# A spectral filter followed by a gated feed-forward network on one core: fifteen blocks of the down-projection rewritten with seven products, and the filter's middle stage re-timed

## The chip, the core and the metric

The kernel runs on one NeuronCore of a Trainium2 chip. TensorE (PE, with its weight loads shown as PEld) multiplies matrices into PSUM, VectorE (DVE), ScalarE (ACT) and GpSimd (POOL) work on tiles, and SyncE (SP) and POOL issue most of the DMAs. The metric is the time of one execution in device microseconds; a lower time is better. The median of three runs of the kernel before is 863.33 us (863.15 to 863.42).

## The reference

Two layers follow each other. The first multiplies the spectrum of each sequence by a filter; the second normalizes every row and applies a gated feed-forward network.

```python
batch, seq, dim = (8, 3008, 256);  n_tokens, d_model, d_ff = (24064, 256, 1536)

X = np.fft.rfft(x, axis=1)
Y = X * (filt_r + 1j * filt_i)[None, :, :]
x = np.fft.irfft(Y, n=3008, axis=1).reshape(24064, 256)

rms = np.sqrt(np.mean(x * x, axis=-1, keepdims=True) + 1e-06)
xn = x / rms * rms_g
g = xn @ w_gate
silu = g * (1.0 / (1.0 + np.exp(-g)))
out = silu * (xn @ w_val) @ w_out
```

## The kernel before

**The feed-forward part sets the frame.** There are 8 sequences `b`, each of 6 blocks `m` of 512 tokens (the last block of a sequence has 384 or 512), and each block takes 12 steps `jt`, one for every 128 columns of d_ff. Such a step is a *slot*; there are 576, numbered through as `items`. In slot `i`, `gv` (L533) makes the gate product in `pg` and the value product in `pv`, each as two accumulating matmuls of 512 columns (L546). ACT applies Silu to `pg` and writes `sg` (L550); DVE multiplies `pv` by `sg` and writes `hh`, 128 d_ff columns by 512 tokens in fp16 (L551). Two slots later `down` (L554) multiplies `hh` by the 128 rows of `wo` of this step: four matmuls, one for each 128 tokens, with the tokens' `hh` as weights and 256 columns of `wo` moving (L563). They accumulate over the 12 steps in two PSUM banks, `po0` and `po1`. After the last step ACT copies one bank and DVE the other to `o3` (L568, L569), and SP stores it. The first `down` of a block is put off by one slot, so that the banks can be emptied.

`pg` and `pv` have two PSUM banks each, `hh` four buffers, `po0` and `po1` one each.

**The filter part runs in the gaps.** For sequence `b` it has these units:

- `x_load` (POOL issues the DMA), `a_unit` (a 512-column matmul into `psa`, copied by ACT or DVE), `z_store` and `t2_load` (SP): the first stage.
- The *middle stage*, sixteen units `i` of each sequence: `b_unit` (four 96-column matmuls into `psb`, L241, and a DVE multiplication by the filter, `s_part`, L231), one slot later the second `s_part` (L234), another slot later `add_unit` (POOL adds both to `ss`, L268); after every second one `yt_load` (a transposing DMA from SP), and some slots later `bi_unit` for both (four 96-column matmuls into `psi`, L285, copied by ACT).
- `t4_load` (SP, transposing), `n_unit` (a 512-column matmul into `psn`, L314, copied by ACT), `sq_unit` (ACT squares and sums, L322), `stat_unit` and `xt_unit` (POOL, L330 to L340), `tr_unit` (SP, transposing) deliver the `xn` of a block.

The first sequence goes through its own start-up, with transposes by TensorE in place of DMAs (`psy`, L418), and one block whose scale is split in two fp16 parts by DVE (`hl`, L509 and L510).

**A planner written in Python sets the order.** For each unit it takes a list of wished slots and `fit` pushes a unit later until the PSUM bank ("M" or "B") is free and the planned loads of ACT ("A") and DVE ("V") leave room. What is planned for a slot is issued behind that slot's `gv` and in front of the `down` of two slots earlier; every engine works through its own queue in that order. For the sequences 3 to 7 the middle stage's wishes are, with `t = (b - 1) * 72`:

```python
b_at, lags, soft = [t - (25 if b == 3 else 26) + 4 * i for i in range(16)], (8, 12), ()
```

The two lags say how many slots behind the `b_unit` the two `bi_unit`s go.

**Staging buffers.** A pool `stg` of four 8 KB buffers per partition holds the filter (`f_load`) and the weights (`w_load`) at the start, and afterwards the `y` tiles of the norm, which use half of a buffer.

Of the kernel before, what the change touches and what calls it, by code (L numbers as in the profile page):

```python
# [10 lines left out]
FP32 = mybir.dt.float32  # L11
FP16 = mybir.dt.float16
AXT = mybir.ActivationFunctionType
ALU = mybir.AluOpType
# [6 lines left out]
P = 128  # L21
D = 256
B = 8
DFF = 1536
JT = DFF // P
# [8 lines left out]
XC = 6  # L34
NXC = H // XC
KC = 8


def _make_tables():
# [62 lines left out]
def kernel(  # L102
# [11 lines left out]
    nc = tc.nc  # L114
# [6 lines left out]
    z_d = nc.dram_tensor("z_tmp", (B, K2, KR, D), FP16, kind="Internal").ap()  # L121

    glob = ctx.enter_context(tc.tile_pool(name="glob", bufs=1))
    stg = ctx.enter_context(tc.tile_pool(name="stg", bufs=4))
    xp = ctx.enter_context(tc.tile_pool(name="xp", bufs=4))
    t1p = ctx.enter_context(tc.tile_pool(name="t1p", bufs=3))
    t2p = ctx.enter_context(tc.tile_pool(name="t2p", bufs=3))
# [7 lines left out]
    hp = ctx.enter_context(tc.tile_pool(name="hp", bufs=4))  # L135
    op = ctx.enter_context(tc.tile_pool(name="op", bufs=2))
# [15 lines left out]
    wg = glob.tile([P, 2, DFF], FP16)  # L152
    wv = glob.tile([P, 2, DFF], FP16)
    wo = glob.tile([P, JT, D], FP16)
    gsb = glob.tile([P, 2], FP32)
    hhs = [glob.tile([P, 512], FP16, name="hh%d" % i) for i in range(4)]
    ss3 = [glob.tile([P, 4, 2, P], FP16, name="ss%d" % i) for i in range(3)]
# [9 lines left out]
    def raw(src, row, ap):  # L167
        return bass.AP(tensor=src.tensor, offset=src.offset + row * D, ap=ap)

    def y_tile():  # L170
        t = stg.tile([P, 2, 4, 256], FP32, tag="stg", name="y")
        return t.rearrange("p a b c -> p (a b c)")[:, 0:1024].rearrange("p (a e) -> p a e", a=2)

    def x_load(b, c):
        t = xp.tile([P, XC, D], FP16, tag="xc", name="xc")
# [195 lines left out]
        copy(eng, st[0]["t2"][c][:, 4 * r:4 * r + 4, :].rearrange("p k (e d) -> p k e d", e=2), ps)  # L371

    fst = {}
    FR4 = 4

    def f_load(i, f):
        if i not in fst:
            fst[i] = stg.tile([P, 2, FR4, D], FP32, tag="stg", name="fs")
        t = fst[i]
        row = FR4 * P * i if i < 2 else NF - 1 - FR4 * P  # L380
        for src in ((filt_i, filt_r)[f],):
            nc.gpsimd.dma_start(t[:, f].rearrange("p a d -> p (a d)"),
                                raw(src, row, [[FR4 * D, P], [1, FR4 * D]]))

    def f_unit(i, f, dh, e):
        t = fst[i]
        ps = bank(1 + "AV".index(e), "psf").rearrange("p (a q) -> p a q", a=FR4)
        for a in range(FR4):
            nc.tensor.transpose(ps[:, a, :], t[:, f, a, ds(dh * P, P)], idf)  # L389
# [123 lines left out]
    def scale_apply(m, bk):  # L513
# [12 lines left out]
                                    in1=y[:, h, :].rearrange("p (q e t) -> p q e t", q=2, e=2), op=ALU.mult)  # L526
        st[0]["xn"][m] = xn

    SPLIT = ((0, 0, 0), (B - 1, 5, JT - 1))
    hh_of = {}  # L530
    po_of = {}

    def gv(b, m, jt):  # L533
        n = nq(b, m)
        xn = st[b]["xn"][m]
        parts = ((0, 2), (2, 4)) if (b, m, jt) in SPLIT else ((0, n),)
        sg = hp.tile([P, 512], FP16, tag="sg", name="sg")
        hh = hhs[(6 * JT * b + JT * m + jt) % 4]
        made = []
        for q0, q1 in parts:  # L540
            w = (q1 - q0) * P
            pg = psG.tile([P, 512], FP32, tag="pg", name="pg")
            pv = psV.tile([P, 512], FP32, tag="pv", name="pv")
            for ps, wt in ((pg, wg), (pv, wv)):
                for dt_ in range(2):
                    nc.tensor.matmul(ps[:, 0:w], wt[:, dt_, ts(jt, P)], xn[:, q0:q1, dt_, :],  # L546
                                     start=(dt_ == 0), stop=(dt_ == 1))
            made.append((pg, pv, w, slice(q0 * P, q1 * P)))
        for pg, pv, w, c in made:
            nc.scalar.activation(out=sg[:, c], in_=pg[:, 0:w], func=AXT.Silu)  # L550
            nc.vector.tensor_tensor(out=hh[:, c], in0=pv[:, 0:w], in1=sg[:, c], op=ALU.mult)  # L551
        hh_of[(b, m, jt)] = hh

    def down(b, m, jt):  # L554
        hh = hh_of.pop((b, m, jt))
        if jt == 0:
            po_of[(b, m)] = [psO.tile([P, 2, D], FP32, tag="po%d" % i, name="po%d" % i)
                             for i in range(2)]
        po = po_of[(b, m)]

        n = nq(b, m)
        for s4 in range(n):
            nc.tensor.matmul(po[s4 // 2][:, s4 % 2, :], hh[:, ts(s4, P)], wo[:, jt, :],  # L563
                             start=(jt == 0 and s4 % 2 == 0),
                             stop=(jt == JT - 1 and (s4 % 2 == 1 or s4 == n - 1)))
# [23 lines left out]

    def w_load(q):  # L590
        cols = ts(q, DFF // 3)
        t = stg.tile([P, 2, 2, DFF // 3], FP32, tag="stg", name="ws")
# [17 lines left out]
    with tc.manual_schedule():  # L610
# [18 lines left out]
        w_load(1)  # L629
        nc.vector.memset(mhalf, -0.5)  # L630
        nc.vector.memset(ones, 1.0)
        for t in ss3[1:]:
# [29 lines left out]
        for g in range(7):  # L662
            tr0_unit(g, "V")
            if g < 6:
                f_unit(*todo[g + 2], "A")
        f_neg(4, 4, (0,))
        f_neg(8, 8, (0,))
        UN = K2 // 2
# [54 lines left out]
        for i in range(JT + 1, len(items), JT):  # L723
            load["A"][i] = 0.6
            load["V"][i] = 0.68

        def at(slot, fn, *a):
            todo = (late if fn == q_unit else plan).setdefault(slot, [])
            if fn in front:
                todo.insert(0, (fn, a))  # L730
            else:
                todo.append((fn, a))
# [77 lines left out]
        for b in range(1, B):  # L810
            t = (b - 1) * 72
            if b == 1:
                z = a_plan(b, [i for i in range(12)])
                b_at, lags = [z + 7 + 7 * i // 5 for i in range(16)], (9, 9)
                soft = range(2, 16, 4)
            elif b == 2:
                z = a_plan(b, [28 + 3 * i for i in range(12)])
                b_at, lags, soft = [z + 13 + 7 * i // 3 for i in range(16)], (8, 9), ()
            else:
                at_ = [72 + 3 * i if b == 3 else t - 87 + 4 * i for i in range(12)]  # L820
                z = a_plan(b, [s - (s % JT == 1) for s in at_])
                b_at, lags, soft = [t - (25 if b == 3 else 26) + 4 * i for i in range(16)], (8, 12), ()
            assert z + 3 <= b_at[0] - 4
            end = b_plan(b, b_at, lags, soft)
            for c in range(4):
                at(end + 1 + (3 * c if b < 3 else c), t4_load, b, c)
            n_at = end + (4, 6, 8)[b] if b < 3 else t + (53 if b == 3 else 51)
            assert n_at >= end + 4
            for m in range(6):
                norm_plan(b, m, (n_at + 8 * m, n_at + 8 * m + (4 if b > 1 else 2)), (2, 3, 7) if b > 1 else (2, 3, 6))  # L830

        for i, now in plan.items():
            if any(fn == a_unit and a[3] == 0 for fn, a in plan.get(i + 1, ())) and bi_unit in [fn for fn, _ in now]:
                now.sort(key=lambda u: u[0] == sq_unit)

        stores = {}
        for i in range(len(items) + 4):
            if i < len(items):
                gv(*items[i])
            for fn, a in plan.pop(i, ()):  # L840
                fn(*a)
            if 2 <= i < len(items) + 2:
                b, m, jt = items[i - 2]
                if jt == 1 and i > JT:
                    down(b, m, 0)
                if jt or i < JT:
                    down(b, m, jt)
                if items[i - 2][2] == JT - 1:
                    stores[i + 1] = items[i - 2][:2]
# [35 lines left out]
```

## Time and profile before

| what | value |
|---|---|
| median of 3 runs (lowest, highest) | 863.33 us (863.15, 863.42) |
| span of the profiled execution, first to last instruction | 861.4 us |
| mean granted TensorE clock in it | 0.999 |
| PE busy | 852.4 us (99%) |
| PEld busy | 532.2 us (62%) |
| ACT busy | 612.4 us (71%) |
| DVE busy | 557.2 us (65%) |
| POOL busy | 297.8 us (35%) |
| blocks 3 of sequences 2 to 6, from first gate matmul to first gate matmul | 16.3 us, in sequence 6 16.1 |
| blocks 4 of sequences 2 to 6 | 16.9, 17.2, 17.2, 16.9, 16.3 us |
| blocks 0 to 4 of sequence 7 | 16.0, 16.3, 15.6, 15.6, 15.6 us |

The span comes from one execution under the profiler, for which no time beside its span is given; the runs' median lies 1.9 us above that span. Busy times are unions over all instructions of an engine; matmuls are pipelined and a record shows a matmul from its start to its modelled end, so the pace of TensorE is read from the starts of successive matmuls. In the groups of instructions a row gives the line, engine, operation, tiles and shapes, the count, busy time and mean nanoseconds of one, and the idle time of the engine in front of them with what ended it. In the timeline a row gives the start and the length in us.

### The profile page before, as it was taken

To read this page: it belongs to the slowest core of one execution; us is meant where nothing else is said; L and a number is where in the kernel's file an instruction comes from. 1 tells how busy PE (TensorE), PEld (TensorE's weight loads), DVE (VectorE), ACT (ScalarE), POOL (GpSimd) and SP (SyncE) were. 2 spreads that over 40 slices of the span, in tenths; PEclk is the share of its full clock that TensorE was granted. 3 is DMA by queue.
4 is the path that set the end of the run, shared out by engine and by line. 5 is a ranking of instruction groups with operands and counts; after the bars stand their busy time and mean duration, and the time that the engine had idled before them with its cause. 6 is when DMAs were issued, how large, how long until landed. Compare 5 with 4: busy or idle time off the path is not lost.

```text
span 861.4 us, 17024 instructions
## 1 busy us (share of the span) xinstructions
PE 852.4 (99%) x6142; PEld 532.2 (62%) x6142; DVE 557.2 (65%) x926; ACT 612.4 (71%) x1339; POOL 297.8 (35%) x346
## 2 busy tenths in 40 slices
PE   8999999999999999999999999999999999999997
PEld 6755666566666666666666666666666666665664
DVE  5857655776666666666666676767666665555554
ACT  4986777787588756887577856888567765777443
POOL 5725742453144322534034430444123430132000
PEclk9999999999999999999999999999999999999999
DMA  9995778765975476656755548433564331521101
GB/s 283 270 204 124 150 164 168 139 130 121 197 137 129 121 150 111 151 107 147 139 127 113 132 98 180 108 87 101 131 127 93 97 70 42 124 54 49 62 25 50
DMA packets 198237, 107.98 MB, mean 125 GB/s; under 512 B 158566, under 2 KB 182520, under 8 KB 198152
## 3 DMA queue, kind: packets, MB, share of 16 engines
q1 hardware_dynamic: 189464, 85.52, 44.1%
q0 software_dynamic: 8544, 21.24, 12.7%
q8 instruction: 48, 0.79, 0.4%
q14 instruction: 37, 0.30, 0.1%
q10 hardware_dynamic: 144, 0.13, 0.0%
HBM read 45.78 MB, written 35.65 MB: 95 GB/s over the span
## 4 chain that ended last, share of the span: by engine, by line
PE 96%; DMA 1%; ACT 1%; DVE 1%; issue 0%; POOL 0%; POOLq 0%
PE po L563 28%; PE pg L546 28%; PE pv L546 28%; PE psb L241 3%; PE psi L285 3%; PE psn L314 2%; PE psa L206 2%; DMA fs<-in_filt_i_dram 1%; PE psy L418 1%; PE psf L389 1%; PE pst L367 0%; ACT sg L550 0%; POOL xc L186 0%; DVE s L231 0%; DVE hh L551 0%
## 5 line engine op out<-in xcount | busy, mean ns | idle before, releaser
L551 DVE TENSOR_TENSOR hh<-pv,sg 128x512 f16<-128x512 f32 (+2 forms) x578 | 391.5, 678 | 286.4 <-ACT sg L550 221.9
L550 ACT ACTIVATE sg<-pg 128x512 f16<-128x512 f32 (+2 forms) x578 | 337.4, 584 | 217.6 <-PE pg L546 213.4
L546 PE MATMUL pg<-xn,wg 128*128 128x512 f16 (+2 forms) x1156 | 338.1, 374 | 0.1
L546 PE MATMUL pv<-xn,wv 128*128 128x512 f16 (+2 forms) x1156 | 338.1, 374 | 0.0
L563 PE MATMUL po<-wo,hh 128*128 128x256 f16 x2256 | 332.7, 273 | 0.0
L563 PEld LDWEIGHTS <-hh 128*128 128x128 f16 x2256 | 213.4, 98 | 105.5 <-issue 0.6
L268 POOL TENSOR_TENSOR ss<-s,s 128x384 f16<-128x384 f16 x112 | 101.9, 911 | 273.2 <-DVE s L234 245.2
L546 PEld LDWEIGHTS <-wv 128*128 128x128 f16 x1156 | 112.9, 98 | 130.7
L546 PEld LDWEIGHTS <-wg 128*128 128x128 f16 x1156 | 111.4, 98 | 17.0 <-issue 0.3
L340 POOL TENSOR_TENSOR xt<-y,rho 128x1024 f16<-128x1024 f32 (+1 forms) x46 | 85.4, 1856 | 2.8
L322 ACT ACTIVATE junk<-y 128x256 f16<-128x256 f32 x180 | 74.3, 413 | 2.8
L231 DVE TENSOR_TENSOR s<-psb,ff 128x384 f16<-128x384 f32 x124 | 67.6, 547 | 0.7 <-ACT ff L195 0.6
L234 DVE TENSOR_TENSOR s<-psb,ff 128x384 f16<-128x384 f32 x124 | 67.6, 546 | 0.0
L195 ACT ACTIVATE uu<-psi 128x384 f16<-128x384 f32 (+1 forms) x127 | 61.6, 486 | 1.5 <-DMA out_dram<-o 0.5
L195 ACT ACTIVATE y<-psn 128x512 f32<-128x512 f32 (+1 forms) x95 | 55.7, 588 | 4.2
L285 PEld LDWEIGHTS <-yt 96*128 96x128 f16 x512 | 35.4, 97 | 26.7 <-issue 1.0
L332 POOL TENSOR_TENSOR rho<-u,mhalf 128x4 f32<-128x4 f32 (+1 forms) x46 | 46.5, 1010 | 3.8
L330 POOL TENSOR_SCALAR u<-ss 128x4 f32<-128x4 f32 (+1 forms) x46 | 8.9, 193 | 104.8 <-ACT junk L322 103.8
L195 ACT ACTIVATE t<-psa 128x512 f16<-128x512 f32 x70 | 41.4, 594 | 3.1 <-PE psa L206 1.7
L285 PE MATMUL psi<-wi,yt 96*128 96x96 f16 x512 | 42.9, 205 | 0.1
L241 PE MATMUL psb<-wb,t 96*128 96x96 f16 x480 | 40.1, 206 | 0.3 <-DVE s L234 0.2
L241 PEld LDWEIGHTS <-t 96*128 96x128 f16 x480 | 28.7, 97 | 12.8 <-DVE s L234 3.3
(101 smaller groups left out, 366.2 us busy)
## 6 DMA issues: line engine op xcount, KB each, us to landing
out_dram<-o SPq DMA_DIRECT2D x40, 512.0 KB, 3.6
xc<-in_x_dram POOLq DMA_DIRECT2D x31, 384.0 KB, 5.6
z_tmp<-t SPq DMA_DIRECT2D x28, 384.0 KB, 2.7
t<-z_tmp SPq DMA_DIRECT2D x28, 384.0 KB, 6.0
out_dram<-o SPq DMA_DIRECT2D x7, 384.0 KB, 2.7
fs<-in_filt_i_dram POOLq DMA_DIRECT2D x3, 512.0 KB, 10.8
fs<-in_filt_r_dram POOLq DMA_DIRECT2D x3, 512.0 KB, 11.2
ws<-in_moe_w_gate_dram POOLq DMA_DIRECT2D x3, 512.0 KB, 9.8
```

The lines of the kernel that those rows point to most:

```text
L195: nc.scalar.activation(out=out, in_=in_, func=AXT.Copy, **({} if scale is None else {"scale": scale}))
L231: eng.tensor_tensor(out=o, in0=ps, in1=f1, op=ALU.mult)
L234: eng.tensor_tensor(out=o, in0=ps[:, :, ::-1, :], in1=f2, op=ALU.mult)
L241: nc.tensor.matmul(ps[:, ts(k, KR)], st[b]["t2"][kk // KC][:, kk % KC, ds(dh * P, P)], wb[0:KR, kk, :], start=True, stop=True)
L268: nc.gpsimd.tensor_tensor(out=ss3[g % 3][:, :, dh, 0:KR], in0=s[0], in1=s[1], op=ALU.add)
L285: nc.tensor.matmul(ps[:, k, :], yt[0:KR, k, dh, :], wi[0:KR, 4 * g + k, :], start=True, stop=True)
L322: nc.scalar.activation(out=junk, in_=y[:, i, ts(u, D)], func=AXT.Square, accum_out=ss[:, 2 * i + u:2 * i + u + 1])
L340: nc.gpsimd.tensor_tensor(out=xt[:, 0:n, :], in0=y.rearrange("p a (u d) -> p (a u) d", u=2)[:, 0:n, :], in1=rho[:, 0:n].unsqueeze(2).to_br ...
L546: nc.tensor.matmul(ps[:, 0:w], wt[:, dt_, ts(jt, P)], xn[:, q0:q1, dt_, :], start=(dt_ == 0), stop=(dt_ == 1))
L550: nc.scalar.activation(out=sg[:, c], in_=pg[:, 0:w], func=AXT.Silu)
L551: nc.vector.tensor_tensor(out=hh[:, c], in0=pv[:, 0:w], in1=sg[:, c], op=ALU.mult)
L563: nc.tensor.matmul(po[s4 // 2][:, s4 % 2, :], hh[:, ts(s4, P)], wo[:, jt, :], start=(jt == 0 and s4 % 2 == 0), stop=(jt == JT - 1 and (s4 ...
```

## The change

Fifteen blocks, `SEVEN`, do their down-projection in another way: blocks 3 and 4 of the sequences 2 to 6, and blocks 0 to 4 of sequence 7. The product of a block is cut in two by two: two tiles of 128 tokens, two tiles of 128 d_ff columns (`j` even and odd) and two halves of the 256 output columns. Instead of eight products of 128 x 128 x 128, Strassen's scheme needs seven, of sums and differences of those tiles.

- `gv_seven` works on 256 tokens (`half`) and two column tiles: the gate and value products have the same number of columns, as four matmuls of 256 columns each in place of two of 512. After `hh`, DVE makes the sums and differences in three additions over 256, 256 and 128 fp16 elements, all from SBUF to SBUF; the first waits for `hh`.
- `down_seven` has seven matmuls of 128 columns in place of four of 256. A half of a block takes six slots. Then ACT copies 128 columns of `pa` and 512 of `pb` to one buffer `osum`, DVE adds the first to 256 columns of `pa`, and POOL makes three additions over 256 fp32 elements. The store is issued two slots later than that of other blocks.
- `w_seven` makes five sums of the weights' tiles on POOL, once each, in slots 96 to 136.
- The new small tiles lie in the unused halves of four fixed buffers `big`, used in turn, which replace the pool `stg`; `w_load(1)` is issued after the loop of `tr0_unit`s.
- The planner counts 0.56 of DVE for each slot of such a block, and some ACT for its drain. The middle stage of the sequences 3 to 7 starts 12 or 13 slots later, and its units follow every three slots instead of every four, with lags 8 and 11. It thereby ends ahead of block 3 of the sequence in whose slots it runs, but for the last `bi_unit`s.

```diff
+    big = [glob.tile([P, 2 * FR4 * D], FP32, name="big%d" % i) for i in range(4)]
+    spare = [t[:, FR4 * D:] for t in big]
...
+    osum = spare[2][:, 384:1024].rearrange("p (s t) -> p s t", s=5)
...
+    SEVEN = {(b, m) for b in range(2, B - 1) for m in (3, 4)} | {(B - 1, m) for m in range(5)}
+
+    def w_seven(n):
...
+        nc.gpsimd.tensor_tensor(out=ws7[n], in0=v[:, :, a[0], a[1], :], in1=v[:, :, b[0], b[1], :], op=f)
+
+    def gv_seven(b, m, jt):
...
+        for ps, wt in ((pg, wg), (pv, wv)):
+            for j in range(2):
+                for dt_ in range(2):
+                    nc.tensor.matmul(ps[:, ts(j, 2 * P)], wt[:, dt_, ts(2 * jp + j, P)],
+                                     xn[:, 2 * half:2 * half + 2, dt_, :], start=(dt_ == 0), stop=(dt_ == 1))
+        nc.scalar.activation(out=sg, in_=pg, func=AXT.Silu)
+        nc.vector.tensor_tensor(out=hh, in0=pv, in1=sg, op=ALU.mult)
+        a = hh.rearrange("p (s t) -> p s t", s=4)
+        n = (6 * JT * b + JT * m + jt) % 4
+        hs, h5 = hs4[n], hs1[n]
+        nc.vector.tensor_tensor(out=hs[:, 0:2], in0=a[:, 0:2], in1=a[:, 3:4].to_broadcast([P, 2, P]), op=ALU.add)
+        nc.vector.tensor_tensor(out=hs[:, 2:4], in0=a[:, 1:3], in1=a[:, 0:4:3], op=ALU.subtract)
+        nc.vector.tensor_tensor(out=h5, in0=a[:, 0], in1=a[:, 2], op=ALU.add)
...
+    def down_seven(b, m, jt):
...
+        mm(pb[:, 0], a[:, 0], ws7[1][:, jp], **first)
+        mm(pb[:, 1], a[:, 3], ws7[2][:, jp], **mid)
+        mm(pa[:, 0], hs[:, 0], ws7[0][:, jp], **first)
+        mm(pb[:, 3], hs[:, 1], w[:, 0, 0], **mid)
+        mm(pa[:, 2], hs[:, 2], ws7[3][:, jp], **mid)
+        mm(pa[:, 1], hs[:, 3], ws7[4][:, jp], **last)
+        mm(pb[:, 2], h5, w[:, 1, 1], **last)
+        if jp == JP - 1:
+            o = o3_of[(b, m)][:, 2 * half:2 * half + 2, :].rearrange("p q (e d) -> p (q e) d", e=2)
+            t = osum
+            nc.scalar.activation(out=t[:, 4], in_=pa[:, 0], func=AXT.Copy)
+            nc.scalar.activation(out=t[:, 0:4], in_=pb, func=AXT.Copy)
+            nc.vector.tensor_tensor(out=o[:, 0:4:3], in0=pa[:, 1:3], in1=t[:, 4:5].to_broadcast([P, 2, P]), op=ALU.add)
+            nc.gpsimd.tensor_tensor(out=o[:, 1:3], in0=t[:, 0:2], in1=t[:, 2:4], op=ALU.add)
+            nc.gpsimd.tensor_tensor(out=t[:, 2:4], in0=t[:, 1::-1], in1=t[:, 2:4], op=ALU.subtract)
+            nc.gpsimd.tensor_tensor(out=o[:, 0:4:3], in0=o[:, 0:4:3], in1=t[:, 2:4], op=ALU.add)
...
+        for b, m in SEVEN:
+            for jt in range(JT):
+                load["V"][6 * JT * b + JT * m + jt] += 0.56
+            load["A"][6 * JT * b + JT * m + JP + 1] += 0.7
...
-                b_at, lags, soft = [t - (25 if b == 3 else 26) + 4 * i for i in range(16)], (8, 12), ()
+                b_at, lags, soft = [t - 13 + 3 * i for i in range(16)], (8, 11), ()
...
+        for n in range(5):
+            at(96 + 10 * n, w_seven, n)
...
+                if jt % n == 1 and i > JT:
+                    fn(b, m, jt - 1)
+                if jt % n or i < JT:
+                    fn(b, m, jt)
+                if jt == JT - 1:
+                    stores[i + (3 if seven else 1)] = (b, m)
```

More of the change, by code (lines that the diff above doesn't have):

```diff
@@ L36 @@
 KC = 8
+FR4 = 4
 def _make_tables():
@@ L123 @@
     glob = ctx.enter_context(tc.tile_pool(name="glob", bufs=1))
-    stg = ctx.enter_context(tc.tile_pool(name="stg", bufs=4))
     xp = ctx.enter_context(tc.tile_pool(name="xp", bufs=4))
@@ L154 @@
     wo = glob.tile([P, JT, D], FP16)
+    big = [glob.tile([P, 2 * FR4 * D], FP32, name="big%d" % i) for i in range(4)]
+    spare = [t[:, FR4 * D:] for t in big]
+    half = [t.bitcast(FP16) for t in spare]
+    ws7 = [half[n // 2][:, ts(n % 2, JT // 2 * P)].rearrange("p (i d) -> p i d", d=P) for n in range(5)]
+    hs4 = [(half[0][:, 1536:], half[1][:, 1536:], half[3][:, 0:512], half[3][:, 512:1024])[i]
+           .rearrange("p (s t) -> p s t", s=4) for i in range(4)]
+    hs1 = [half[3][:, 1024 + i * P:1024 + (i + 1) * P] for i in range(4)]
+    osum = spare[2][:, 384:1024].rearrange("p (s t) -> p s t", s=5)
     gsb = glob.tile([P, 2], FP32)
@@ L168, in raw, with big_tile @@
         return bass.AP(tensor=src.tensor, offset=src.offset + row * D, ap=ap)
+    turn = [0]
+    def big_tile():
+        turn[0] += 1
+        return big[(turn[0] - 1) % 4]
     def y_tile():
-        t = stg.tile([P, 2, 4, 256], FP32, tag="stg", name="y")
-        return t.rearrange("p a b c -> p (a b c)")[:, 0:1024].rearrange("p (a e) -> p a e", a=2)
+        return big_tile()[:, 0:FR4 * D].rearrange("p (a e) -> p a e", a=2)
     def x_load(b, c):
@@ L373 @@
     fst = {}
-    FR4 = 4
     def f_load(i, f):
         if i not in fst:
-            fst[i] = stg.tile([P, 2, FR4, D], FP32, tag="stg", name="fs")
+            fst[i] = big_tile().rearrange("p (f a d) -> p f a d", f=2, a=FR4)
         t = fst[i]
@@ L527, in scale_apply @@
         st[0]["xn"][m] = xn
+    JP = JT // 2
+    SEVEN = {(b, m) for b in range(2, B - 1) for m in (3, 4)} | {(B - 1, m) for m in range(5)}
+    def w_seven(n):
+        v = wo.rearrange("p (i j) (e d) -> p i j e d", j=2, e=2)
+        f, a, b = ((ALU.add, (0, 0), (1, 1)), (ALU.subtract, (0, 1), (1, 1)), (ALU.subtract, (1, 0), (0, 0)),
+                   (ALU.add, (0, 0), (0, 1)), (ALU.add, (1, 0), (1, 1)))[n]
+        nc.gpsimd.tensor_tensor(out=ws7[n], in0=v[:, :, a[0], a[1], :], in1=v[:, :, b[0], b[1], :], op=f)
@@ new lines, in gv_seven @@
+    def gv_seven(b, m, jt):
+        half, jp = divmod(jt, JP)
+        xn = st[b]["xn"][m]
+        sg = hp.tile([P, 512], FP16, tag="sg", name="sg")
+        hh = hhs[(6 * JT * b + JT * m + jt) % 4]
+        pg = psG.tile([P, 512], FP32, tag="pg", name="pg")
+        pv = psV.tile([P, 512], FP32, tag="pv", name="pv")
+        for ps, wt in ((pg, wg), (pv, wv)):
[11 more added lines that the diff above has]
+        nc.vector.tensor_tensor(out=h5, in0=a[:, 0], in1=a[:, 2], op=ALU.add)
+        hh_of[(b, m, jt)] = (a, hs, h5)
@@ new lines, in down_seven @@
+    def down_seven(b, m, jt):
+        a, hs, h5 = hh_of.pop((b, m, jt))
+        half, jp = divmod(jt, JP)
+        if jt == 0:
+            o3_of[(b, m)] = op.tile([P, 4, D], FP32, tag="o3", name="o3")
+        if jp == 0:
+            po_of[(b, m)] = [psO.tile([P, 2, D], FP32, tag="po%d" % i, name="po%d" % i)
+                             .rearrange("p a (e d) -> p (a e) d", e=2) for i in range(2)]
+        pa, pb = po_of[(b, m)]
+        first, mid, last = dict(start=(jp == 0), stop=False), dict(start=False, stop=False), \
+            dict(start=False, stop=(jp == JP - 1))
+        w = wo[:, 2 * jp:2 * jp + 2, :].rearrange("p j (e d) -> p j e d", e=2)
+        mm = nc.tensor.matmul
+        mm(pb[:, 0], a[:, 0], ws7[1][:, jp], **first)
[14 more added lines that the diff above has]
+            nc.gpsimd.tensor_tensor(out=o[:, 0:4:3], in0=o[:, 0:4:3], in1=t[:, 2:4], op=ALU.add)
+            po_of[(b, m)] = o3_of[(b, m)]
@@ L529 @@
     SPLIT = ((0, 0, 0), (B - 1, 5, JT - 1))
+    o3_of = {}
     hh_of = {}
@@ L591, in w_load @@
         cols = ts(q, DFF // 3)
-        t = stg.tile([P, 2, 2, DFF // 3], FP32, tag="stg", name="ws")
+        t = big_tile().rearrange("p (k e j) -> p k e j", k=2, e=2)
         for src, k in ((moe_w_gate, 0), (moe_w_val, 1)):
@@ L628 @@
         w_load(0)
-        w_load(1)
         nc.vector.memset(mhalf, -0.5)
@@ L665 @@
                 f_unit(*todo[g + 2], "A")
+        w_load(1)
         f_neg(4, 4, (0,))
@@ L838 @@
             if i < len(items):
-                gv(*items[i])
+                (gv_seven if items[i][:2] in SEVEN else gv)(*items[i])
             for fn, a in plan.pop(i, ()):
@@ L843 @@
                 b, m, jt = items[i - 2]
[L844 to L849, printed above, removed]
+                seven = (b, m) in SEVEN
+                fn, n = (down_seven, JP) if seven else (down, JT)
+                if jt % n == 1 and i > JT:
[4 more added lines that the diff above has]
+                    stores[i + (3 if seven else 1)] = (b, m)
             for fn, a in late.pop(i, ()):
```

## The prediction

> **What bounds the kernel now.** I read the engine shares and the clock on the page, then the chain of waits, to see which engine sets the end.
>
> ```profile
> PE 852.4 (99%) x6142; PEld 532.2 (62%) x6142; DVE 557.2 (65%) x926; ACT 612.4 (71%) x1339; POOL 297.8 (35%) x346
> ...
> PEclk9999999999999999999999999999999999999999
> ...
> PE 96%; DMA 1%; ACT 1%; DVE 1%; issue 0%; POOL 0%; POOLq 0%
> PE po L563 28%; PE pg L546 28%; PE pv L546 28%; PE psb L241 3%; PE psi L285 3%; PE psn L314 2%; PE psa L206 2%; DMA fs<-in_filt_i_dram 1%; PE psy L418 1%; PE psf L389 1%; PE pst L367 0%; ACT sg L550 0%; POOL xc L186 0%; DVE s L231 0%; DVE hh L551 0%
> ```
>
> TensorE holds 96% of the chain at a clock that never drops, and po, the product that changes, is 28%. A busy share is an average, so I next asked the windows view for five stretches: two blocks of sequence 3 that change (m 3 and 4), the one behind them, and of sequence 7 block 2 and blocks 3 and 4.
>
> ```profile
> 409.60:425.90 16.30, 16.30 (x115) 10.07 (x113) 9.83 (x16) 9.18 (x16) 1.20 (x2) 1.00 0.61 122
> 425.90:443.00 17.10, 17.10 (x118) 10.39 (x116) 11.74 (x20) 11.76 (x26) 5.86 (x6) 1.00 0.64 135
> 443.00:461.00 18.00, 18.00 (x129) 11.05 (x128) 12.35 (x21) 14.62 (x34) 6.42 (x7) 1.00 0.70 154
> 792.90:808.70 15.80, 15.80 (x101) 9.55 (x99) 8.79 (x14) 9.02 (x18) 3.09 (x3) 1.00 0.18 51
> 808.70:839.90 31.20, 31.20 (x195) 18.77 (x193) 17.80 (x27) 15.52 (x26) 0.00 (x0) 1.00 0.09 34
> ```
>
> Columns: length, then busy time of PE, PEld, DVE, ACT, POOL, clock, DMA. PE is busy in all of every stretch: a nanosecond taken from PE here is a nanosecond off the end, and any new wait of PE is paid in full. Two blocks without other work take 31.20 us, so a bare slot is 1.300 us. The timeline gives its parts:
>
> ```profile
> 815.18 0.59 PE L546 MATMUL pg<-xn,wg 128*128 128x512 f16 x2
> 815.61 0.59 PE L546 MATMUL pv<-xn,wv 128*128 128x512 f16 x2
> 815.81 0.60 ACT L550 ACTIVATE sg<-pg 128x512 f16<-128x512 f32 x1 [0.70 <-PE pg L546]
> 816.04 0.60 PE L563 MATMUL po<-wo,hh 128*128 128x256 f16 x4
> 816.44 0.69 DVE L551 TENSOR_TENSOR hh<-pv,sg 128x512 f16<-128x512 f32 x1 [0.61 <-ACT sg L550]
> 816.48 0.59 PE L546 MATMUL pg<-xn,wg 128*128 128x512 f16 x2
> ```
>
> From start to start, two 512-column matmuls take 0.43 us and four 256-column ones 0.44. Over all starts of the timeline a po matmul takes 0.1093 us and a 512-column one 0.2157.
>
> **PE's part of the change.** The nearest row for a 128-column matmul with a fresh weight each is the first sequence's psy:
>
> ```profile
> 27.96 0.61 PE L418 MATMUL psy<-tab,s 128*96 128x128 f16 x8
> 28.41 0.25 PE L285 MATMUL psi<-wi,yt 96*128 96x96 f16 x2
> ```
>
> Eight in 0.45 us are 0.056 us each. Gate and value in halves: 8 x 0.1093 - 4 x 0.2157 = +0.012 us a slot. Down: 7 x 0.056 - 4 x 0.1093 = -0.045. Sum -0.034 us a slot, 180 slots: **-6.2 us**. The slot becomes 1.266 us.
>
> The Trainium skill (TensorE: Matmul & The Clock Gate, Back-to-back issue gap) says that in a stream of weight loads and matmuls N=128 takes about 81 ns. By it the slot would grow by 7 x 0.025 - 0.034 = 0.14 us and the sum be +25 us (an estimate); the psy row, itself such a stream, shows 56, so I go by the row.
>
> **VectorE's part.** What DVE does today, from the groups with shapes apart and from the timeline of the first blocks:
>
> ```profile
> L551 DVE TENSOR_TENSOR hh<-pv,sg 128x512 f16<-128x512 f32 x526 | 363.3, 691 | 265.9 <-ACT sg L550 207.3 <-PE psn L314 28.9 <-PE psa L206 13.4
> L231 DVE TENSOR_TENSOR s<-psb,ff 128x384 f16<-128x384 f32 x124 | 67.6, 547 | 0.7 <-ACT ff L195 0.6
> ```
>
> ```profile
> 55.31 0.16 DVE L509 CAST hl<-rho 128x4 f16<-128x4 f32 x1
> 55.50 0.16 DVE L510 TENSOR_TENSOR hl<-rho,hl 128x4 f16<-128x4 f32 x1
> 55.58 0.68 DVE L197 CAST t<-psa 128x512 f16<-128x512 f32 x1
> ```
>
> L510 reads what L509 wrote: it starts 0.03 us after L509's end; the first sum waits for hh in the same way, and queued behind it is the next hh, which frees pv for PE. Independent neighbours overlap instead (hh to s 0.608 us start to start, s to hh 0.464). So hh and its first sum are 0.691 + 0.035 = 0.726 us apart. The three sums are SBUF only and fp16, which no row shows in this size. The 16-bit copy from PSUM of 96x1024 takes 687 ns, what 512 fp32 elements take: two elements a cycle. At two, 256 elements are 0.133 us, plus a fixed part: 0.064 (s) to 0.076 (L510, 0.08 start to start), so three sums cost 0.525 to 0.56 us; at one a cycle, 0.86. I take 0.54, between the first two, as every operand is 16-bit and unit-stride: DVE needs 1.266 us a slot, exactly PE's. On top, each half block drains with a 256-element add, 0.35 us (L569's 256-column form, 0.365; hh's, 0.341). A block costs DVE 12 x 1.266 + 0.70 = 15.9 us.
>
> PE per block afterwards, from slots plus the other units that the planner leaves there (0.17 for four psi or psb matmuls, 0.216 for psn or psa): m 3 of sequences 2 to 6, 15.7; m 4, 15.8 to 16.2, where one s pair adds 0.46 to DVE's 15.9; sequence 7, 15.8, 15.8, then 15.2 three times. DVE's excess over PE: 5 x 0.2 (m 3) + 1.3 (m 4, 0.1 to 0.4 each) + 2 x 0.1 + 3 x 0.7 = 4.6 us. Not all is lost: hh and its sums run a slot ahead of the down matmuls, some 0.3 us of lag at the drain, once for each of six stretches: 1.8 given back. Loss 2.8 us. With sums of 0.525 a block is 15.7 and the loss about 1; with 0.56 it is 16.1 and about 5.
>
> **ACT, POOL, SP.** ACT's two copies a half (about 0.17 and 0.48 start to start, against one of 0.48 a block) push the next sg to 1.4 us after the last down matmul; DVE's drain add, which waits for the first copy and holds up the next hh, ends its slot at 1.6, so the copies hide behind it. ACT has 5 to 7 us free in the first two stretches; I allow 0.2 us in all. POOL gains three 256-element fp32 adds a half. From xt (128x1024 1,893 ns, 128x768 1,466) 256 elements extrapolate to 0.61 us, from 997 at 128x384 to 0.78: 0.7 taken, 2.3 us a half with gaps, in 7.6 us; POOL is nearly empty there (1.2 us of 16.3). ACT's next copy of pb waits for the last of them through the one osum; 5 us of room cover it, and without that room sg, queued behind, would stop PE. The output store on SP waits for it too, with transposes queued behind; it is emitted two slots later, and psi comes five slots (6.5 us) behind a transpose that lands in 3.2. The five weight sums on POOL (about 1.5 us each by xt's 128x768) hold back an add at most 1.5 us under the same cover. If that cover is gone, psi waits on PE for the remainder.
>
> **The middle stage** keeps its work: b_unit, two s, one add on POOL, transposes on SP, bi_unit, t2 and t4 loads. At three slots ACT reaches 12.4 us and DVE 11.6 in an 18.2 us block, POOL 9.6. The 443.0 stretch ran with ACT at 14.6 of 18.0 and PE never idle, so I put it at 0; the upper end is 2 us, three DVE pieces of 0.7 on the chain in sequences 0 and 1, where the lanes were as tight. The w_load that moves keeps its place on POOL's queue: 0.
>
> **Sum** against the profiled 861.4: -6.2 + 2.8 + 0.2 (drain delays) = -3.2, so a span of 858.2. The median, 863.33, lies 1.9 above the span; I keep that: 860.1.
>
> **Rivals.**
> - *The sums collide with POOL (slower).* Today every large DVE operation reads PSUM and at most one SBUF tensor. The sums read two, while POOL reads two for its adds; no row shows both at once. The cost is from nothing to a whole POOL op. In the 2.3 us of a half's three adds DVE reaches its sums about twice; half an op (0.35) twice would be 0.7 us, one whole op each 1.4. As DVE has no slack, it decides from 3.2/30 = 0.11 us a half. I price 0.45: 30 x 0.45 = 13.5, so 873.6; at 0.7, 881; at 1.4, 902. For: all sums and adds share the same stretches. Against: all of POOL's drains fit into a third of the time. The Trainium skill (SBUF — State Buffer, Who interferes with whom) says that a DVE instruction with two SBUF inputs and a GpSimd one that reads SBUF exclude each other, the second blocked until the first finishes; no run here shows it yet. By it this rival is the outcome.
> - *DVE eats it (same).* Sums at 0.56 or a longer wait behind hh lose 5 to 6 us: 862 to 863.3. The middle stage's 2 us would end there too.
> - *DVE does not bind.* Sums under 0.5: the full -6.2, 857.1.
> - *One element a cycle.* Slots of 1.59 us, 15 blocks of 19.7 against 245 us for the 15 today: +50, 914. The PSUM copy speaks against it.
> - *Weight loads bind the short matmuls.* A load of 128x128 lasts 98 ns (PEld, L563); exposed in each of seven, the slot grows by 0.26 us: +47, 910. Against it, psy's loads last 123 ns at 56 ns from start to start.
>
> **How the numbers follow.** A measurement of this kernel tells about 0.2% (1.7 us) from no change: faster is under 861.6, slower over 865.1. Chances: the forecast 0.40, DVE not binding 0.08 (both faster); all eaten 0.17 (same); collision 0.27; one element a cycle 0.05; weight loads 0.03 (slower). Faster 0.48, same 0.17, slower 0.35. The likeliest case alone spans 858.3 (sums at 0.525) to 861.6. The range starts at 856.8, just under the full saving, and reaches up to 875, past the collision's price, leaving its dearer half out.
>
> **What the next profile would show.** PE: seven down matmuls 0.056 apart, else the PE term is wrong. DVE: sums near 0.29, 0.29 and 0.22 us long (start to start 0.2, 0.2, 0.13); over 0.4 is one element a cycle; sums that are long only where POOL is at its drain adds are the collision. Blocks 2 to 4 of sequence 7 should be DVE-bound, near 15.9 us against 15.6 now; blocks 3 of sequences 2 to 6 near 15.8 against 16.3. PE idle behind DVE elsewhere, or psi waiting for a transpose, would prove the middle stage's zero wrong.

## The result, and the profile after

The change makes the kernel slower: 890.13 us median (889.97 to 890.48, 4 runs) against 863.24 (863.15 to 863.42, 4 runs), a ratio of 1.0311 with a 95% interval of 1.0297 to 1.0326. The profiled execution spans 888.7 us against 861.4. The forecast was 860.1 with a range up to 875, so both are missed.

The page of the kernel after, its engine shares and its chain of waits by engine and by line:

```profile
PE 856.1 (96%) x7402; PEld 603.0 (68%) x7402; DVE 683.4 (77%) x1475; ACT 622.7 (70%) x1390; POOL 374.7 (42%) x441
...
PE 71%; DVE 19%; issue 4%; DMA 2%; ACT 1%; SPq 1%; POOL 1%; DVEq 0%; POOLq 0%
PE po L638 18%; PE pv L621 17%; PE pg L621 17%; DVE hh L563 8%; DVE big L568 5%; DVE big L569 3%; PE pg L560 3%; PE pv L560 3%; PE psb L254 3%; PE psi L298 2%; PE psa L219 2%; PE psn L327 2%; DMA big<-in_filt_i_dram 1%; DVE big L567 1%; DVE o L597 1%
```

PE fell from 96% of the chain to 71%, and DVE rose from 1% to 19%: hh (L563) and the three sums behind it (L567 to L569, whose tiles lie in `big`) now stand on the path. The windows view says in which blocks (length, then busy time of PE, PEld, DVE, ACT, POOL, clock, DMA; sequence 3's m 4, then block 2 and blocks 3 and 4 of sequence 7):

```profile
430.90:448.70 17.80, 16.66 (x192) 14.70 (x190) 17.35 (x52) 11.96 (x28) 6.96 (x9) 1.00 0.72 149
...
812.90:831.70 18.80, 15.97 (x185) 14.17 (x183) 18.39 (x50) 9.70 (x21) 7.78 (x9) 1.00 0.15 43
831.70:867.10 35.40, 30.97 (x364) 28.32 (x362) 34.57 (x100) 16.96 (x32) 9.29 (x12) 1.00 0.08 31
```

Here DVE is busy nearly all the time and PE is not; before, PE filled every such stretch. The last two blocks take 35.40 us where they took 31.20. From the first gate matmul of a block to the next one's, the fifteen blocks took 244.8 us before and take 262.6 now.

The groups of DVE's three sums, shapes apart (busy time, mean ns):

```profile
L567 DVE TENSOR_TENSOR big<-hh 128x256 f16<-128x256 f16 x180 | 65.9, 366 | 6.2
L568 DVE TENSOR_TENSOR big<-hh 128x256 f16<-128x256 f16 x180 | 58.7, 326 | 0.0
L569 DVE TENSOR_TENSOR big<-hh 128x128 f16<-128x128 f16 x180 | 49.3, 274 | 0.0
```

The means hide two kinds. The timeline of PE, DVE and POOL in sequence 7 (start, length, engine, line) shows both:

```profile
818.35 0.72 POOL L600 TENSOR_TENSOR o<-o,big 128x256 f32<-128x256 f32 x1
818.65 0.56 DVE L567 TENSOR_TENSOR big<-hh 128x256 f16<-128x256 f16 x1
819.03 1.94 POOL L353 TENSOR_TENSOR xt<-big,rho 128x1024 f16<-128x1024 f32 x1
819.14 1.98 DVE L568 TENSOR_TENSOR big<-hh 128x256 f16<-128x256 f16 x1
821.04 0.21 DVE L569 TENSOR_TENSOR big<-hh 128x128 f16<-128x128 f16 x1
...
822.34 0.22 PE L585 MATMUL po<-big,hh 128*128 128x128 f16 x1
822.40 0.22 PE L586 MATMUL po<-big,hh 128*128 128x128 f16 x1
...
827.05 0.78 POOL L599 TENSOR_TENSOR big<-big 128x256 f32<-128x256 f32 x1
827.16 0.81 DVE L568 TENSOR_TENSOR big<-hh 128x256 f16<-128x256 f16 x1
```

A sum beside nothing on POOL takes what was forecast: 292, 283 and 217 ns, 0.209, 0.201 and 0.135 us from start to start, 0.545 in all. A sum that starts while POOL works on one of its drain adds or on xt, both of which read SBUF, lasts until 80 to 150 ns after that operation's end: 0.56 us behind a drain add, 1.98 us behind an xt. In the whole trace 62 of the 540 sums are long, by 31.3 us together: 53 of them by 19.8 us beside the 90 drain adds (L598 to L600), 9 of them by 11.5 us beside xt (L353). The two PE lines show the seven products at the forecast pitch, 0.06 us.

Added over the timeline, PE's gaps (a matmul that starts later behind its predecessor than that one's columns take) grew from 13.5 us to 46.9. Of the 33.4 us more, 26.5 lie in the fifteen blocks, 5.3 in the blocks behind them (m 5 of sequences 2 to 6) and some 1.5 in sequences 1 and 3, beside the middle stage. Less the 6.2 that the products save, that is about the 27.3 us of the span. The view of waits names DVE's drain add, not a long sum, as releaser of most of it:

```profile
PE po L587 <- DVE o L597: 14.9, 24, 1.1
```

L587 is the first matmul of a half that writes `pa`, the bank that the drain add L597 empties, and also the first that needs a sum. L597 stands in DVE's queue behind whatever delay the sums before it have gathered, so the view's releaser is where that delay reaches PE. That the sums are the cause is for the experiments to show.

### The profile page after: what moved, and what is told of

Same layout as the page of the kernel before. It is cut to its first block, busy times and chain, and to the rows that moved or that the text cites. A ratio compares the mean times of both kernels' runs of the same rounds, so it can differ in the third digit from the quotient of the medians.

```text
span 888.7 us, 20284 instructions
## 1 busy us (share of the span) xinstructions
PE 856.1 (96%) x7402; PEld 603.0 (68%) x7402; DVE 683.4 (77%) x1475; ACT 622.7 (70%) x1390; POOL 374.7 (42%) x441
## 4 chain that ended last, share of the span: by engine, by line
PE 71%; DVE 19%; issue 4%; DMA 2%; ACT 1%; SPq 1%; POOL 1%; DVEq 0%; POOLq 0%
PE po L638 18%; PE pv L621 17%; PE pg L621 17%; DVE hh L563 8%; DVE big L568 5%; DVE big L569 3%; PE pg L560 3%; PE pv L560 3%; PE psb L254 3%; PE psi L298 2%; PE psa L219 2%; PE psn L327 2%; DMA big<-in_filt_i_dram 1%; DVE big L567 1%; DVE o L597 1%
## 5 line engine op out<-in xcount | busy, mean ns | idle before, releaser
L626 DVE TENSOR_TENSOR hh<-pv,sg 128x512 f16<-128x512 f32 (+2 forms) x398 | 267.1, 672 | 176.8 <-ACT sg L625 136.0
L625 ACT ACTIVATE sg<-pg 128x512 f16<-128x512 f32 (+2 forms) x398 | 230.4, 580 | 127.9 <-PE pg L621 124.9
L621 PE MATMUL pv<-xn,wv 128*128 128x512 f16 (+2 forms) x796 | 230.7, 371 | 1.1 <-DVE hh L626 0.9
L621 PE MATMUL pg<-xn,wg 128*128 128x512 f16 (+2 forms) x796 | 230.8, 371 | 0.1
L638 PE MATMUL po<-wo,hh 128*128 128x256 f16 x1536 | 227.1, 272 | 0.0
L562 ACT ACTIVATE sg<-pg 128x512 f16<-128x512 f32 x180 | 107.5, 597 | 98.7 <-PE pg L560 45.2
L563 DVE TENSOR_TENSOR hh<-pv,sg 128x512 f16<-128x512 f32 x180 | 122.8, 682 | 4.0 <-ACT sg L562 3.9
L560 PE MATMUL pv<-xn,wv 128*128 128x256 f16 x720 | 108.0, 272 | 1.4 <-DVE hh L563 0.7
L560 PE MATMUL pg<-xn,wg 128*128 128x256 f16 x720 | 108.0, 273 | 0.0
L353 POOL TENSOR_TENSOR xt<-big,rho 128x1024 f16<-128x1024 f32 (+1 forms) x46 | 85.7, 1863 | 2.7
L560 PEld LDWEIGHTS <-wv 128*128 128x128 f16 x720 | 70.4, 98 | 11.2 <-issue 2.8
L567 DVE TENSOR_TENSOR big<-hh 128x256 f16<-128x256 f16 x180 | 65.9, 366 | 6.2
L598 POOL TENSOR_TENSOR o<-big 128x256 f32<-128x256 f32 x30 | 22.8, 761 | 110.7 <-ACT big L596 110.7
```

The costliest lines, as they stand in the source:

```text
L353: nc.gpsimd.tensor_tensor(out=xt[:, 0:n, :], in0=y.rearrange("p a (u d) -> p (a u) d", u=2)[:, 0:n, :], in1=rho[:, 0:n].unsqueeze(2).to_br ...
L560: nc.tensor.matmul(ps[:, ts(j, 2 * P)], wt[:, dt_, ts(2 * jp + j, P)], xn[:, 2 * half:2 * half + 2, dt_, :], start=(dt_ == 0), stop=(dt_ = ...
L562: nc.scalar.activation(out=sg, in_=pg, func=AXT.Silu)
L563: nc.vector.tensor_tensor(out=hh, in0=pv, in1=sg, op=ALU.mult)
L567: nc.vector.tensor_tensor(out=hs[:, 0:2], in0=a[:, 0:2], in1=a[:, 3:4].to_broadcast([P, 2, P]), op=ALU.add)
```

## The experiments

My theory was that the sums stand still while POOL reads SBUF. The rival was that the boundary of the half blocks is slow by itself: the seven-product drain, its two ACT copies and its DVE add.

**e1_write_only: POOL's three drain adds become fills.** The outputs of the fifteen blocks are left unfinished.

```diff
-            nc.gpsimd.tensor_tensor(out=o[:, 1:3], in0=t[:, 0:2], in1=t[:, 2:4], op=ALU.add)
-            nc.gpsimd.tensor_tensor(out=t[:, 2:4], in0=t[:, 1::-1], in1=t[:, 2:4], op=ALU.subtract)
-            nc.gpsimd.tensor_tensor(out=o[:, 0:4:3], in0=o[:, 0:4:3], in1=t[:, 2:4], op=ALU.add)
+            nc.gpsimd.memset(t[:, 0:5], 0.0)
+            nc.gpsimd.memset(t[:, 0:5], 0.0)
+            nc.gpsimd.memset(o[:, 1:3], 0.0)
+            nc.gpsimd.memset(o[:, 0:4:3], 0.0)
```

> POOL's three drain additions of each half block are replaced by four fills of the same tiles (the output of the fifteen blocks is left unfinished): POOL is busy at the same places but reads nothing from SBUF. Collision (a DVE sum with two SBUF inputs stands still while POOL executes an operation that reads SBUF): in the profile of the change 53 sums that lie on these additions are 19.8 us too long and 9 that lie on xt 11.5 us; the first go, the second stay, so about 890 - 20 = 870 us. Boundary (the wait sits in the drain itself: two ACT copies, a DVE addition and one pair of PSUM banks, whatever POOL does): within 2 us of 890. POOL merely busy beside DVE: also about 890.

Measured 874.56 us, ratio 1.013 (1.0115 to 1.0145), span 872.8. POOL's occupation was kept (four fills of 0.63, 0.63, 0.31 and 0.31 us a half), yet 15.9 us of span went. The timeline of DVE and POOL:

```profile
816.36 0.63 POOL L598 MEMSET big<- 128x640 f32 x1 [5.80 <-DVE o L597]
816.87 0.29 DVE L567 TENSOR_TENSOR big<-hh 128x256 f16<-128x256 f16 x1
817.05 0.63 POOL L599 MEMSET big<- 128x640 f32 x1
817.08 0.28 DVE L568 TENSOR_TENSOR big<-hh 128x256 f16<-128x256 f16 x1
```

Sums that overlap a fill keep their length; the only long ones left are nine beside xt, now by 15.3 us. PE's gaps in the fifteen blocks fall from 26.5 to 9.4 us. The boundary rival asked for 888 to 890 and falls, and so does the idea that a POOL merely busy beside DVE is enough. The time is 4.6 us above the 870 expected: beside xt the long sums grew from 11.5 to 15.3 us, so all long sums together fell by 16.0 us, as the span did.

**e2_write_only_xt_act: as e1, and the nine xt on ACT.**

```diff
+        if (b > 2 and m == 0) or (b == B - 1 and m > 1):
+            for q in range(n):
+                nc.scalar.activation(out=xt[:, q, :], in_=y.rearrange("p a (u d) -> p (a u) d", u=2)[:, q, :],
+                                     func=AXT.Copy, scale=rho[:, q:q + 1])
+        else:
...
```

> As the first, and the nine xt scalings that fall into the rewritten blocks are made by ACT (four scaled copies of 256 columns each) in place of POOL. Collision: nothing on POOL reads SBUF beside the sums any more, all 62 long sums go, and what is left is the sum of the forecast without the collision: 890.1 - 31.3 = 858.8, at most 861. Boundary: about 888 to 890. Balance (DVE's own 15.9 us a block against PE's): 858 to 863, which would leave the collision as the only other term.

Measured 872.69 us, ratio 1.0106 (1.0089 to 1.0123), span 871.0. No sum is long any more, as the groups of the three sums show (in this kernel lines L572 to L574):

```profile
L572 DVE TENSOR_TENSOR big<-hh 128x256 f16<-128x256 f16 x180 | 52.6, 292 | 6.2
L573 DVE TENSOR_TENSOR big<-hh 128x256 f16<-128x256 f16 x180 | 51.2, 284 | 0.0
L574 DVE TENSOR_TENSOR big<-hh 128x128 f16<-128x128 f16 x180 | 39.3, 218 | 0.0
```

But the time fell by only 1.9 us: the edit brought a wait of its own. ACT works in order, and its xt copies wait for POOL's rho with the next Silu behind them (timeline, ACT and POOL):

```profile
751.87 1.08 POOL L345 TENSOR_TENSOR rho<-u,mhalf 128x4 f32<-128x4 f32 x1
752.99 1.71 ACT L355 ACTIVATE xt<-big,rho 128x256 f16<-128x256 f32 x4 [1.49 <-POOL rho L345]
754.60 0.57 ACT L567 ACTIVATE sg<-pg 128x512 f16<-128x512 f32 x1
```

So as a time it missed. What it does show is the seven-product block by itself, where that wait is absent: 15.83 us for m 3 of sequences 2 to 6, and 16.08, 15.85 and 15.84 for blocks 2 to 4 of sequence 7. The last two, in which PE has no other work, bear the forecast's 15.9 out; m 3 says little, as it takes 15.78 even without the sums (e3).

**e3_no_sums: the three sums left out.** The matmuls read zeros in their place.

```diff
-        nc.vector.tensor_tensor(out=hs[:, 0:2], in0=a[:, 0:2], in1=a[:, 3:4].to_broadcast([P, 2, P]), op=ALU.add)
-        nc.vector.tensor_tensor(out=hs[:, 2:4], in0=a[:, 1:3], in1=a[:, 0:4:3], op=ALU.subtract)
-        nc.vector.tensor_tensor(out=h5, in0=a[:, 0], in1=a[:, 2], op=ALU.add)
```

> DVE's three sums a slot are left out (the five products that need them take zeros); all matmuls, drains and POOL's additions stay. Collision and balance: DVE has no SBUF-only operation left, PE keeps its saving of 6.2 us whole: 857. Boundary: the waits of PE at the first sum's matmul of each half (0.4 to 1.3 us, some 20 us in all) stay: about 877. Weight loads bind the short matmuls: over 863.

Measured 858.93 us, ratio 0.9949 (0.9934 to 0.9964), span 858.4. PE's gaps in the fifteen blocks are 0.0, with all of POOL's adds, ACT's copies and the boundary in place. Blocks 2 to 4 of sequence 7 go from 15.60 us before to 15.17, 0.036 a slot where 0.034 was forecast. The time is 2 us above the 857 expected. That the span is not 855 comes for the most part from outside the blocks: the first gate matmul starts 1.5 us later, and a psb waits 1.3.

**e4_middle_only: the kernel before, with the middle stage at the new slots.**

```diff
-                b_at, lags, soft = [t - (25 if b == 3 else 26) + 4 * i for i in range(16)], (8, 12), ()
+                b_at, lags, soft = [t - 13 + 3 * i for i in range(16)], (8, 11), ()
```

> The kernel before with the middle stage of sequences 3 to 7 moved as in the change, no block rewritten. The forecast's zero for this part: 863.3, within 1 us. If the denser middle stage by itself makes PE wait (the profile of the change has 6.7 us more of PE waits in blocks that are not rewritten): up to 870.

Measured 864.44 us, ratio 1.0013 (1.0003 to 1.0022), span 862.3, or +0.9. The first unit of sequence 3's middle stage waits for its t2 load (psb, 0.57 us of PE's gap), and sequence 3 adds 0.17 and 0.14. The move is nearly free, not quite.

**e5_ten_blocks: seven products without sequence 7.**

```diff
-    SEVEN = {(b, m) for b in range(2, B - 1) for m in (3, 4)} | {(B - 1, m) for m in range(5)}
+    SEVEN = {(b, m) for b in range(2, B - 1) for m in (3, 4)}
```

> The change with sequence 7 left as before: ten rewritten blocks in place of fifteen. Collision: in the profile of the change the five blocks of sequence 7 take 92.1 us against 79.1 before, four xt and ten drains of POOL beside the sums; so 890.1 - 13 = 877. Balance alone (DVE's 15.9 us a block, no collision) would make those five blocks only 0.3 us longer than 79.1 and leave about 889.5.

Measured 877.33 us, ratio 1.0163 (1.0146 to 1.018), as expected. Gaps in the ten blocks are 11.2 us and long sums 18.0 us (12.4 beside drain adds, 5.6 beside xt). Of the 26.9 us that the change loses, the ten blocks have 14.1 and the five of sequence 7 the other 12.8.

**e8_copies: one SBUF input on POOL instead of two.** The three adds become copies of the same size; the output of the fifteen blocks is unfinished.

```diff
-            nc.gpsimd.tensor_tensor(out=o[:, 1:3], in0=t[:, 0:2], in1=t[:, 2:4], op=ALU.add)
-            nc.gpsimd.tensor_tensor(out=t[:, 2:4], in0=t[:, 1::-1], in1=t[:, 2:4], op=ALU.subtract)
-            nc.gpsimd.tensor_tensor(out=o[:, 0:4:3], in0=o[:, 0:4:3], in1=t[:, 2:4], op=ALU.add)
+            nc.gpsimd.tensor_copy(out=o[:, 1:3], in_=t[:, 0:2])
+            nc.gpsimd.tensor_copy(out=t[:, 2:4], in_=t[:, 0:2])
+            nc.gpsimd.tensor_copy(out=o[:, 0:4:3], in_=t[:, 2:4])
```

> The change with fifteen blocks, POOL's three additions of each half replaced by three copies of 256 elements: POOL reads one SBUF tensor in place of two (the output of these blocks is left unfinished). If any read of POOL blocks the sums: long sums stay, shorter as the copies are (128x128 f16 took 0.29 us, so perhaps 0.4 each): 874.6, the fills' time, plus 5 to 8: about 880. If only a POOL operation with two SBUF inputs blocks: 874.6. Boundary: 890.

Measured 880.77 us, ratio 1.0202 (1.0187 to 1.0217), span 878.3. Copies of 0.40 us, half the length of an add, still stop 36 sums, for 5.8 us, and xt costs 15.3. The timeline of DVE and POOL:

```profile
810.05 0.39 POOL L598 COPY o<-big 128x256 f32<-128x256 f32 x1
810.07 0.52 DVE L568 TENSOR_TENSOR big<-hh 128x256 f16<-128x256 f16 x1
810.39 0.46 POOL L599 COPY big<-big 128x256 f32<-128x256 f32 x1
810.51 0.41 DVE L569 TENSOR_TENSOR big<-hh 128x128 f16<-128x128 f16 x1
```

One SBUF read on POOL's side is enough. The Trainium skill (SBUF — State Buffer, Who interferes with whom) states this: a DVE instruction with two SBUF inputs contends with a GpSimd one that reads SBUF, not with one that only writes it, and the port pair that they share is an exclusive lock. The traces agree: adds and copies stop the sums (53 and 36 of them), fills stop none, and hh, with one SBUF input, keeps its 0.68 us beside any of them.

**e6_ten_no_reads: ten blocks, fills, and the norm a few slots later,** so that xt falls behind the blocks.

```diff
-            n_at = end + (4, 6, 8)[b] if b < 3 else t + (53 if b == 3 else 51)
+            n_at = end + (4, 6, 8)[b] if b < 3 else t + 54
```

> Ten rewritten blocks, POOL's drain additions replaced by fills (the output of these blocks is left unfinished), and the norm of sequences 3 to 7 one to three slots later, so that its xt falls behind the rewritten blocks and stays on POOL. No operation of POOL that reads large SBUF tiles is left beside the sums. Collision: -4.1 from PE, about +1.2 where DVE needs 15.9 us a block, +1.1 for the middle stage as measured alone: 861.5. The first experiments' rest (9 us left when all long sums were gone) would here be shown to come from xt on ACT, which waits for POOL. If that rest is instead something of the rewritten blocks' own (boundary), it stays: 866 to 868.

Measured 870.72 us, ratio 1.0084 (1.0069 to 1.0099), a miss by 9 us. The ten blocks now wait only 1.6 us and no sum is long, so no collision is left. One new wait, in the view of waits, and SP's timeline and the windows around it:

```profile
PE psi L298 <- DMA yt<-ss: 6.6, 1, 6.6
...
350.06 1.62 SPq L362 DMA_TRANSPOSE xn<-xt  x1
351.76 1.49 SPq L288 DMA_TRANSPOSE yt<-ss  x1
...
362.00:369.00 7.00, 6.83 (x33) 3.68 (x34) 2.50 (x5) 3.88 (x10) 0.91 (x1) 0.57 0.72 113
```

The later norm put a transpose of xn into SP's queue just ahead of the yt that psi needs. That yt then took 10.4 us from issue to landing, where those of the kernel before took 3.2 in the median and 4.8 at most, and psi started on it at 362.18. Beside it an x load was under way, issued by POOL at 352.07, which took 9.1 us (the x load nearest to it in e5 took 4.9). That these transfers held each other up is likely, but no run separates them. Behind PE's pause the granted clock was 0.57 from 362 to 369 us, which costs some 3 us more (7 us times 0.43). Without the two the span of 869.4 would be near 860, by this estimate.

**e7_deferred_adds: a whole version.** Ten blocks; ACT copies pb straight into the output tile, DVE makes one sum from PSUM, and POOL's twelve adds of a sequence run in slots 62 to 73, behind its two blocks. The norm comes as late as in e6, the stores come later, and `sg` has three buffers.

```diff
-            nc.scalar.activation(out=t[:, 4], in_=pa[:, 0], func=AXT.Copy)
-            nc.scalar.activation(out=t[:, 0:4], in_=pb, func=AXT.Copy)
-            ...
+            nc.scalar.activation(out=t4, in_=pa[:, 0], func=AXT.Copy)
+            nc.scalar.activation(out=o, in_=pb, func=AXT.Copy)
+            nc.vector.tensor_tensor(out=q, in0=pa[:, 1:3], in1=t4.unsqueeze(1).to_broadcast([P, 2, P]), op=ALU.add)
+            later[(b, m, half)] = (o, q)
...
+        for b in range(2, B - 1):
+            for k in range(12):
+                at(72 * b + 62 + k, drain_add, b, 3 + k // 6, k // 3 % 2, k % 3)
```

> Ten rewritten blocks with their whole output: ACT copies pb straight into the output tile, DVE's 256 sums of pa go to a small buffer of each half, and POOL makes the three additions of all four halves in the block behind, where DVE has no sums; norm later as in the run before; sg has three buffers in place of four. Collision: as that run, 861.5, so faster than the kernel before by about 0.2% and than the change by 28 us. If POOL's 9 us of additions there hold up the middle stage of the next sequence: psi waits on PE, 863 to 866.

Measured 863.91 us, ratio 1.0007 (0.9998 to 1.0016): no change that can be told. The blocks wait 1.4 us. Three gaps elsewhere took the rest: psb 0.92 (the t2 load, as in e4), and psi 0.72 and 1.49. The yt of these two is issued as soon as POOL's `ss` ends (at 360.11 and 563.57 us), and `ss` stands in POOL's queue behind an xt and the drain adds.

**e9_spread_adds: the same, with those three waits aimed at.** The adds are spread over 17 slots, the stores follow later, and sequence 3's first t2 loads come eight slots earlier.

```diff
-            for k in range(12):
-                at(72 * b + 62 + k, drain_add, b, 3 + k // 6, k // 3 % 2, k % 3)
+            for k, s in enumerate((62, 63, 65, 66, 66, 68, 71, 72, 74, 75, 77, 78)):
+                at(72 * b + s, drain_add, b, 3 + k // 6, k // 3 % 2, k % 3)
...
-                at(slots[0] - 4 + c if c < 3 else slots[4] + 1, t2_load, b, c)
+                at(slots[0] - (12 if b == 3 else 4) + c if c < 3 else slots[4] + 1, t2_load, b, c)
```

> The kernel of e7_deferred_adds (seven products in ten blocks, the whole output, POOL's twelve additions per sequence moved behind the two blocks) with its three remaining waits aimed at: the twelve additions are spread over 17 slots instead of 12, keeping clear of the slots with POOL's add_unit, the two stores follow later, and the first three t2 loads of sequence 3 are issued eight slots earlier. If the theory is whole (the change loses only by the sums that stand still and by queues that its additions delay), the waits of 0.92, 0.72 and 1.49 us of e7_deferred_adds go and its span of 862.0 falls to 858.9, a time of about 860.8 us, 0.3% under the kernel before, with the seven-product blocks still waiting 1.4 us. If the freed time only turns up in another queue (POOL's sums of the middle stage, or the stores that now meet the next sequence's transposes on SP), it stays at 863 to 864 us.

Measured 860.92 us (860.75 to 861.49, 9 runs) against 863.17, ratio 0.9974 (0.9964 to 0.9984), span 859.2. This version beats both kernels, the one before by 0.26%; 860.8 was expected. In the page, engine shares and the chain by engine:

```profile
PE 849.0 (99%) x6982; PEld 579.1 (67%) x6982; DVE 619.0 (72%) x1289; ACT 621.4 (72%) x1376; POOL 347.3 (40%) x411
...
PE 93%; POOL 2%; DMA 2%; ACT 1%; DVE 1%; issue 1%; POOLq 0%
```

PE holds the chain again. The gaps of 0.92 and 1.49 us are gone; the psi of 0.71 us stayed. The ten blocks still wait 1.45 us, DVE's excess over PE.

## Why the prediction was wrong, step by step

**PE's part, -6.2: right.** The products run 0.06 us apart in the trace after, and e3 saves 0.036 us a slot, 6.4 us over 180 slots. (The forecast's own 0.034 a slot makes 6.1, not 6.2.) The 81 ns of the Trainium skill (TensorE: Matmul & The Clock Gate, Back-to-back issue gap) did not appear in this stream of loads and matmuls.

**VectorE's slot, 0.726 + 0.54: right.** Unblocked sums take 0.545, the gap behind hh is 0.035, and a block that only DVE bounds takes 15.85 us (e2) against the 15.9 forecast.

**The loss by balance, 2.8: somewhat low.** In e9 ten blocks wait 1.45 us; in e2 blocks 2 to 4 of sequence 7 take 0.91, 0.68 and 0.67 us more than in e3, and its block 0 takes 0.4. That is 4.1 us, near the 4.6 before the "1.8 given back"; in sequence 7, with 2.7 against 2.3 forecast, nothing was given back.

**The middle stage, 0: off by 1 us,** inside its bound of 2. Its cost was not the DVE pieces that the bound was made of but a t2 load that came late (e4), and an earlier load removes the wait (e9).

**ACT and the drain: right.** With no sums to hold up (e3), the fifteen blocks have no gap at all behind ACT's two copies, POOL's adds or the output stores.

**The sums collide with POOL: the step that failed.** The mechanism, its place and its sign were written down, but as a rival, with a chance of 0.27 and a price of 13.5 us; in the sum of the forecast it stood at nothing. The runs leave 28.6 us for it. Three things were wrong in it.

- *The likelihood.* The argument against it was that the drains fill only a third of the time. That is no protection. On DVE a slot is 0.726 us of hh and then 0.54 us of sums. An add of 0.73 to 0.79 us is as long as the stretch without sums. Of the 90 adds, 18 come behind the last half of a run of blocks, where no sums follow; every one of the other 72 overlapped a sum, and 53 sums were held up. The decision point of 0.11 us a half was far below what one caught sum costs.
- *The price beside the adds.* It was 0.45 us a half; 19.8 us over 30 halves are 0.66, near the 0.7 that was priced at 881.
- *The other reader.* Only the adds of the change were counted. POOL's xt, there before and untouched, reads SBUF for 1.9 us. Nine of them fall into the fifteen blocks, and each one catches a sum, for 11.5 us in all. POOL was called nearly empty from one block (1.2 us of 16.3 in sequence 3's m 3); m 4 of the same sequence showed 5.86 us in the same view.

The account closes: the span grew by 27.3 us; with -6.4 for PE, 4.1 for balance and about 1 for the middle stage, 28.6 us are left for the collision, whose long sums add up to 31.3. That the other 2.7 ended in slack is the difference of the two, not measured by itself.

## What to carry to other kernels

Before giving DVE an operation with two SBUF inputs, list every POOL operation in the same stretches that reads SBUF, the old ones too, and where DVE has no slack price each by how long it lasts. Here an xt of 1.9 us lengthened the sums by 1.3 to 1.7 us, an add of 0.73 by 0.22 in the mean and a copy of 0.40 by 0.06. Moving the readers behind the stretch helped most: ten blocks went from 877.3 us (e5) to 863.9 (e7). Then look at every in-order queue that the moved work passes: here transposes on SP (e6) and copies on ACT (e2) gave back much of what had been freed.

## What the runs showed of the hardware

- A DVE sum of two SBUF tensors that starts inside a large POOL operation that reads SBUF ends 80 to 150 ns after that operation; 0.28 us became up to 1.98. A copy with one input does it as an add does; a fill does not. POOL's rho, 1.0 us long on four elements, lengthened no sum.
- Beside the sums POOL's add L599 lasted 788 ns in the mean, up to 866; the same size lasted 725 in e9, apart from the sums. Both sides pay, the longer operation little.
- A pause of PE of 6.6 us was followed by 7 us at a granted clock of 0.57 (e6); the gaps of up to 1.3 us in the stretches shown of the kernel after left the clock at 1.00.
